# Attention beside a long convolution on one core: other steps for VectorE's share of the softmax, and a paced convolution

## The chip, the cores and the metric

The kernel runs on one core of one Trainium2 chip. The time is the device time of one execution in microseconds. Shown is the median of several runs and one profiled execution with its trace.

## What is computed

Two independent parts share a launch; their outputs stand side by side, each [2048, 512].

```python
# part A: attention, S = 2048, D = 512, 32 heads of 16
q, k, v = split_heads(x @ wqkv)
p = softmax((q @ k.T) * 16 ** -0.5)      # per head, 2048 x 2048
a = merge_heads(p @ v) @ wo

# part B: a gated long convolution, 512 channels, length 2048
kv = (sum over t of shifted(k, t) * shift_k[:, t]) * v
y = causal_conv(kv, ssm_k)               # per channel, written with FFTs
y = y + kv * ssm_D
b = q * y

out = concat([a, b], axis=-1)
```

## The kernel before, in words

Five instruction streams (PE, ScalarE or ACT, VectorE or DVE, GpSimd or POOL, and SP) are written out by a Python loop over steps `T`. Each engine runs its stream in order; semaphores tie them together. What the loop emits in which step is therefore the order of each queue; the steps are no clock.

**Attention.** Scores are made in blocks of 128 keys by 512 queries for one head. Four heads make a group, so a group is 64 blocks (16 key tiles by 4 heads), and 32 groups (4 blocks of queries by 8) make the whole. A step takes three blocks (two in some early steps): `emit_qk(T)` (matmul at line 487) writes them to PSUM banks 0-2 or 3-5 in turn, and one ScalarE instruction (line 494) takes the exponential of all three into a slot of `PT`. There are 692 steps, 21.33 to a group. In a later step `emit_pv` (line 559) multiplies the exponentials with the values and sums into bank 6. After a group's last block `finish_group` copies the sum out (`OF`, line 584), turns it (586), and in the next two steps makes the reciprocal (592), turns back (593) and multiplies into `OTN` (599).

**VectorE's share.** From the fifth group on (group 4, step 94), four blocks of each group are not done by ScalarE. `DVE_AT` says in which steps of the group, as two pairs: the third block of such a step is left to VectorE, and ScalarE takes two. VectorE reads the bank right away (`exp_on_dve`, line 512, the "fix", into `EI`), which frees it. Both blocks of a pair are then carried through a polynomial together: `split` (lines 516 and 518), `horner` three times (523) and `last` (528, into `PTD`). These five items are put into `dve_fill`, each with a step in which it is due, and the loop emits them ahead of the background work of that step. The matmuls on `PTD` are emitted six steps after the second block of the pair.

**Background.** In each step `emit_bg` adds one piece of other work to PE, all of it in bank 7. It is one of: a part of a q projection (24 units of two steps, evacuated by line 321), a part of an output projection (12 jobs of three steps, evacuated by line 639), or a stretch of the convolution. The convolution of four channels (a "quad") is 16 lags of four small matmuls (line 679) against `WR`, windows of the reversed filter that are read from a scratch in HBM (`load_wr`, 512 KB a channel, issued on SP's queue). `WR` holds 12 channels, three quads; a quad's slots are loaded anew when its last lag is emitted. After four quads the bank is copied to `YB` (695); after eight, `conv_turn` transposes and multiplies with the gate (706 and 715), and after 32 the gated result is stored by POOL's queue. There are 128 quads, 2048 lags.

Up to `LAGS` = 5 lags go into a step. A hand-made estimate decides whether the next window can be there: `now(T)` gives a time for the step, `st["wr"]` holds the time at which each quad's loads should have landed, and while that isn't reached the step gets no lag. Between groups of four quads one or more jobs are started; a started job takes its steps before any lag.

```python
    def now(T):
        t1 = N_EARLY + 30
        return 12.0 + 1.36 * min(T, t1) + 1.28 * max(T - t1, 0)
```

`bank_free[b]` holds the instruction that last emptied bank `b`; whoever writes the bank next waits for it.

Of the kernel before, what the change touches and what calls it, by code (L numbers as in the profile page):

```python
# [35 lines left out]
LAGS = 5  # L36
# [7 lines left out]
QSCALE = SCALE * math.log2(math.e) * OCT  # L44
FIX_LO = -118.0 * OCT
FIX_ADD = (math.log2(C4) - 1.0) * OCT
DVE_AT = ((2, 4), (10, 12))


class Eng:  # L50
# [41 lines left out]
def bass_concat_heads__mha_block__ssm_conv_h3__prompt_kernel(  # L92
# [165 lines left out]
    bank_free = {b: None for b in range(8)}  # L258
# [166 lines left out]
    chunks = []  # L425
    b_ = 0
    while b_ < NBLK:
        T = len(chunks)
# [34 lines left out]
    dve_pv = {}  # L463
    for n in range(2, NQB * NG):
        t0 = chunk_of[first[n]][0]
        if t0 < N_EARLY + 30:
            continue
        for pair in DVE_AT:
            for t in pair:
                on_dve[chunks[t0 + t][0][2]] = len(on_dve)  # L470
                dve_pv[chunks[t0 + t][0][2]] = t0 + pair[1] + 6

    h_exp = {}
    h_blk = {}
# [32 lines left out]
    def exp_on_dve(b, bank, h, T):  # L507
        i = on_dve[b]
        p = i // 2
        m = EM[:, :, :].bitcast(FP32)  # L510
        st = {}
        h_fix[i] = dve.op(lambda e: e.tensor_scalar(EI[:, i % 2, :], PS[:, bank, :], FIX_LO, FIX_ADD, ALU.max, ALU.add),  # L512
                          [h, h_pair.get(p - 1)])

        def split():
            st["m"] = dve.op(lambda e: e.tensor_scalar(EM[:, :, :], EI[:, :, :], 0x7fffff, 0x3f800000,  # L516
                                                       ALU.bitwise_and, ALU.bitwise_or), [h_fix[i], h_fix[i - 1]])
            st["e"] = dve.op(lambda e: e.tensor_scalar(EI[:, :, :], EI[:, :, :], 0x7f800000, 0x40000000,  # L518
                                                       ALU.bitwise_and, ALU.bitwise_xor), [st["m"]])

        def horner(j):
            src = m if j == 0 else EH[:, :, :]
            st["h"] = dve.op(lambda e: e.scalar_tensor_tensor(EH[:, :, :], src, (B3, B2, B1)[j], m, ALU.add, ALU.mult),  # L523
                             [st["m"], st.get("h")])

        def last():
            h_pair[p] = h_blk[b] = h_blk[b1] = dve.op(
                lambda e: e.scalar_tensor_tensor(PTD[:, :, :], EH[:, :, :], B0, EI[:, :, :].bitcast(FP32),  # L528
                                                 ALU.add, ALU.mult), [st["h"], st["e"], h_ptd.get(p - 1)])
        if i % 2:  # L530
            b1 = blk_on_dve[i - 1]
            dve_fill.extend([(T + 1, split), (T + 2, lambda: horner(0)), (T + 3, lambda: horner(1)),
                             (T + 4, lambda: horner(2)), (T + 5, last)])
        return h_fix[i]

    blk_on_dve = {i: b for b, i in on_dve.items()}
    dve_fill = []
# [130 lines left out]
    def conv_lags(qd, n0, n1):  # L668
        kk = qd % 8
        deps = [h_wr[4 * qd + c] for c in range(4)] + [h_kvc[0]]  # L670
        if kk % 4 == 0 and n0 == 0:
            deps.append(bank_free[BGB])

        def fn(e):
            ins = None
            for n in range(n0, n1):
                for c in range(4):
                    d = 4 * qd + c
                    ins = e.matmul(PS[32 * c:32 * c + NB - n, BGB, 128 * (kk % 4):128 * (kk % 4) + 128],  # L679
                                   lhsT=KV[:, n:NB, d],  # L680
                                   rhs=WR[:, d % R_W, 128 * (NB - 1 - n):128 * (NB - n)],
                                   start=(n == 0), stop=(n == NB - 1), tile_position=(0, 32 * c))
            return ins
        h = pe.op(fn, deps)
        if n1 == NB:
            for c in range(4):
                h_wrfree[4 * qd + c] = h
                if 4 * qd + c + R_W < C:
                    load_wr(4 * qd + c + R_W)
            if kk % 4 == 3:  # L690
                half = kk // 4
                src = PS[:, BGB, :]
                src = bass.AP(tensor=src.tensor, offset=PS[:, BGB, 127:128].offset,
                              ap=[src.ap[0], [128, 4], [-1, 128]])
                hh = dve.op(lambda e: e.tensor_copy(YB[:, half, :].rearrange("p (k i) -> p k i", k=4), src),  # L695
                            [h, h_yb[0]])
                bank_free[BGB] = hh
        return h
# [28 lines left out]
    for o in range(1, 4):  # L727
# [1 line left out]
    later_q = [("q", qb, g) for qb in range(1, NQB) for g in range(NG)]  # L729
    later_op = [(qb, t) for qb in range(NQB - 1) for t in range(4)]  # L730
    state = {"early": 0, "qd": 0, "lag": 0, "turn": False, "q": 0, "op": 0, "job": [], "gap": 0, "started": False,
             "wr": [], "dma": 0.0}

    def now(T):
        t1 = N_EARLY + 30
        return 12.0 + 1.36 * min(T, t1) + 1.28 * max(T - t1, 0)

    def group_step(qb, g):
        return NT * (qb * NG + g) // (NQB * NG)
# [13 lines left out]
    def emit_bg(T):  # L753
        st = state
        if st["early"] < len(early):
            if T % 3 == 2 and T >= 16:
                return
            unit(early[st["early"]], 5 if T < N_EARLY - 1 else 7)
            st["early"] += 1
            return  # L760
        if not kv_pieces and not st["started"]:
            st["started"] = True
            st["dma"] = now(T) + 18.0
            for i in range(R_W // 4):
                st["wr"].append(st["dma"] + 1.5)
            load_wop(pe_last())
            for d in range(R_W):
                load_wr(d)
            for i in range(2):
                load_qn(i, [h_kvc[0], h_kzt[0]])  # L770
            return
        if st["turn"]:
            conv_turn(st["qd"] // 8 - 1)
            st["turn"] = False
            st["gap"] = 0
            return
        if not st["started"]:
            return
        if st["job"]:
            st["job"].pop(0)()  # L780
            return
        if st["qd"] % 4 == 0 and st["lag"] == 0:
            ready = st["qd"] < C // 4 and st["wr"][st["qd"]] <= now(T)
            urgent = st["q"] < len(later_q) and T + 60 > group_step(*later_q[st["q"]][1:])
            if st["gap"] < 1 or urgent or not ready:
                if not urgent and st["op"] < len(later_op) and (later_op[st["op"]][0] * NG + NG - 1) in h_otn:
                    start_job(op_job(*later_op[st["op"]]))
                    st["op"] += 1
                    return
                if st["q"] < len(later_q):  # L790
                    u = later_q[st["q"]]
                    if T >= group_step(u[1] - 2, u[2]) + 30:
                        start_job(unit_job(u))
                        st["q"] += 1
                        return
        left = LAGS
        while left and st["qd"] < C // 4 and st["wr"][st["qd"]] <= now(T) and not st["turn"]:
            n0 = st["lag"]
            n1 = min(n0 + left, NB)
            left -= n1 - n0  # L800
            conv_lags(st["qd"], n0, n1)
            st["lag"] = n1 % NB
            if n1 == NB:
                st["qd"] += 1
                for i in range(4):
                    st["dma"] = max(st["dma"], now(T) + 3.0) + 1.3
                st["wr"].append(st["dma"] + 1.5)
                if st["qd"] % 4 == 0:
                    st["gap"] = 0
                    st["turn"] = st["qd"] % 8 == 0  # L810
                    break

    def pe_last():
        return (pe.sem, pe.n)
# [3 lines left out]
    for b in range(NBLK):  # L818
        qb, g, kt, s = blk(b)
        n = qb * NG + g  # L820
        t = dve_pv[b] if b in on_dve else chunk_of[b][0] + 2
        if n >= 2:
            t = max(t, chunk_of[last_blk[n - 1]][0] + 3)
        pv_at.setdefault(t, []).append(b)

    for T in range(NT + 3):
        if T < NT:
            emit_qk(T)
        if T == NT:
            op_mm(NQB - 1, 0, 0, 7, BGB)  # L830
            op_mm(NQB - 1, 1, 0, 7, chunks[NT - 2][1][0])
        pvs = pv_at.get(T, [])
        while pvs:
            emit_pv(pvs[:4], T)
            pvs = pvs[4:]
        for item in list(dve_fill):
            if item[0] <= T:
                dve_fill.remove(item)
                item[1]()
        emit_bg(T)  # L840
        for item in list(dve_later):
            if item[0] <= T:
                dve_later.remove(item)
                item[1]()
        for _ in range(1 if T < 3 else 0 if T < 9 else 1 if T < N_EARLY else 2):
            if kv_pieces:
                kv_pieces.pop(0)()
# [65 lines left out]
```

## Time and profile before

| | |
|---|---|
| median of 3 runs | 970.77 us (970.12 to 973.75) |
| profiled execution | 970.83 us, span 969.0 us |
| granted PE clock, mean | 0.933 |
| ScalarE busy | 898.0 us (93%) |
| PE busy (matmul rows) | 780.4 us (81%) |
| VectorE busy | 653.8 us (67%) |
| DMA read from HBM | 287.31 MB, 303 GB/s over the span |

How to read the lines that follow: a row of the timeline has its start and its length in us, the engine, the line of the kernel, the operation, output<-input, the count of instructions that were merged, and in brackets the idle time before it with what ended it. A row of the waits has who waited, `<-` for whom, the total in us, how often, and the longest. A row of the groups has after the bar the busy time in us and the mean length of one in ns, then the idle time before. PE is the matmul, PEld the weight load. PE's granted clock is 1.00 at full speed.

### The profile page before, as it was taken

The numbers are of one execution on the slowest core, as the hardware profiler recorded it, in microseconds if no ns is written. First come the engines' busy times: TensorE is split into PE (matmuls) and PEld (weight loads), VectorE is DVE, ScalarE is ACT, GpSimd is POOL, SyncE is SP. The second block draws the span as 40 slices with busy tenths as digits, with TensorE's granted clock in tenths as the row PEclk, the third lists the DMA queues.
The fourth block names the chain that finished last, engine by engine and source line by source line (L and its number), as shares of the span: only waits on it lengthen the run. The fifth ranks groups of instructions, "written<-read, shape, count | busy, mean of one in ns | idle before, by whom it ended". The sixth has DMA issues, their size and how long they took to land.

```text
span 969.0 us, 28338 instructions
## 1 busy us (share of the span) xinstructions
PE 780.4 (81%) x12851; PEld 341.5 (35%) x12892; DVE 653.8 (67%) x834; ACT 898.0 (93%) x699; POOL 46.7 (5%) x65
## 2 busy tenths in 40 slices
PE   8998887887777877777778777777777788787888
PEld 3322123433333433334334333343333334343212
DVE  3678825766776766776775676667786767677664
ACT  4788898999999999999999989999999999999995
POOL 2011410000000100000001000000000000000000
PEclk8999798999999999999998999999999999999656
DMA  9533399998989999989999989999999999998100
GB/s 315 179 110 109 87 303 357 362 372 338 367 328 349 359 367 364 369 334 384 354 365 346 358 322 347 347 361 360 346 381 349 344 354 350 373 397 349 22 1 22
DMA packets 88570, 295.59 MB, mean 305 GB/s; under 512 B 11269, under 2 KB 19458, under 8 KB 88066
## 3 DMA queue, kind: packets, MB, share of 16 engines
q1 hardware_dynamic: 82114, 280.13, 77.0%
q0 software_dynamic: 3936, 12.58, 4.1%
q8 instruction: 102, 1.67, 0.7%
q10 hardware_dynamic: 2400, 1.05, 0.4%
q14 instruction: 18, 0.15, 0.0%
HBM read 287.31 MB, written 6.42 MB: 303 GB/s over the span
## 4 chain that ended last, share of the span: by engine, by line
ACT 37%; DVE 34%; PE 20%; DMA 5%; issue 3%; SPq 1%; ACTq 0%
ACT PT L494 36%; DVE EH L523 10%; DMA WR<-kz_scratch 5%; PE PS L487 5%; PE PS L559 4%; PE PS L679 3%; DVE EI L512 3%; DVE PTD L528 3%; DVE EI L518 2%; PE PS L631 2%; DVE EM L516 2%; PE PS L307 2%; DVE DT L586 2%; DVE OF L584 2%; DVE OTN L599 2%
## 5 line engine op out<-in xcount | busy, mean ns | idle before, releaser
L494 ACT ACTIVATE PT<-PS 128x1536 bf16<-128x1536 f32 (+1 forms) x692 | 892.8, 1460 | 53.4 <-PE PS L487 51.4
L487 PE MATMUL PS<-QT,KTo 32*128 32x512 bf16 x2048 | 287.4, 409 | 108.1 <-ACT PT L494 101.6
L679 PE MATMUL PS<-WR,KV 128*8 128x128 bf16 (+15 forms) x8192 | 298.5, 227 | 25.2 <-DMA WR<-kz_scratch 11.4
L559 PE MATMUL PS<-PT,VAF 128*32 128x512 bf16 x1936 | 306.2, 414 | 2.0 <-issue 0.7
L679 PEld LDWEIGHTS PS<-WR,KV 128*14 128x14 bf16 (+15 forms) x8192 | 195.9, 107 | 57.7 <-issue 42.0
L512 DVE TENSOR_SCALAR EI<-PS 128x512 int32<-128x512 f32 x112 | 78.1, 698 | 144.8 <-PE PS L487 141.9
L487 PEld LDWEIGHTS PS<-QT,KTo 32*128 32x128 bf16 x2048 | 67.9, 91 | 280.7 <-ACT PT L494 217.6
L523 DVE SCALAR_TENSOR_TENSOR EH<-EH,EM 128x1024 f32<-128x1024 f32 x112 | 139.8, 1249 | 3.5
L559 PEld LDWEIGHTS PS<-PT,VAF 128*32 128x32 bf16 x1936 | 69.3, 94 | 161.4 <-issue 151.1
L528 DVE SCALAR_TENSOR_TENSOR PTD<-EH,EI 128x1024 bf16<-128x1024 f32 x56 | 70.4, 1258 | 1.6
L523 DVE SCALAR_TENSOR_TENSOR EH<-EM 128x1024 f32<-128x1024 f32 x56 | 70.7, 1262 | 0.0
L584 DVE COPY OF<-PS 128x512 f32<-128x512 f32 x30 | 20.5, 685 | 46.9 <-PE PS L559 39.7
L293 PE MATMUL PS<-xT,WQP 128*128 128x512 bf16 x109 | 35.3, 405 | 9.1 <-DVE QN L715 3.8
L518 DVE TENSOR_SCALAR EI<-EI 128x1024 int32<-128x1024 int32 x56 | 39.9, 713 | 1.9
L516 DVE TENSOR_SCALAR EM<-EI 128x1024 int32<-128x1024 int32 x56 | 40.2, 718 | 1.1
L695 DVE CAST YB<-PS 128x512 bf16<-128x512 f32 x32 | 21.8, 682 | 28.2 <-PE PS L679 20.9
L631 PE MATMUL PS<-WKV,OTN 128*128 128x512 bf16 x115 | 33.9, 408 | 8.1 <-DVE QN L715 2.9
L559 PE MATMUL PS<-PTD,VAF 128*32 128x512 bf16 x112 | 24.3, 430 | 19.9 <-DVE PTD L528 19.7
L321 DVE TENSOR_SCALAR QT<-PS 128x512 bf16<-128x512 f32 x32 | 21.9, 686 | 26.6 <-PE PS L293 26.6
L169 POOL DMA_DIRECT2D out_dram<-OUTA x12 | 6.6, 551 | 369.6 <-DVE OUTA L639 369.6
L593 DVE STREAM_TRANSPOSE DT<-DR 128x512 f32<-128x512 f32 x31 | 22.4, 723 | 1.1
L169 POOL DMA_DIRECT2D out_dram<-QN x4 | 4.7, 1171 | 382.1 <-DVE QN L715 382.1
(66 smaller groups left out, 299.3 us busy)
## 6 DMA issues: line engine op xcount, KB each, us to landing
WR<-kz_scratch SPq DMA_DIRECT2D x512, 512.0 KB, 8.4
WR<-in_B_k_dram POOLq DMA_DIRECT2D x16, 256.0 KB, 4.9
kz_scratch<-WR SPq DMA_DIRECT2D x1, 2176.0 KB, 8.9
KV<-in_A_x_dram SPq DMA_DIRECT2D x4, 512.0 KB, 6.7
QN<-in_B_q_dram POOLq DMA_DIRECT2D x4, 512.0 KB, 11.3
out_dram<-QN POOLq DMA_DIRECT2D x4, 512.0 KB, 8.0
WR<-in_B_v_dram SPq DMA_DIRECT2D x6, 256.0 KB, 3.2
QT<-in_B_k_dram POOLq DMA_DIRECT2D x6, 256.0 KB, 4.2
```

The source lines that it names most:

```text
L293: return e.matmul(PS[:, bank, :], lhsT=WQP[:, dc, g, :], rhs=xT[:, dc, qb * 512:(qb + 1) * 512], start=(dc == 0), stop=(dc == 3))
L487: ins = e.matmul(PS[:, bank, :], lhsT=KTo[32 * s:32 * s + 32, g // 2, kt * 128:(kt + 1) * 128], rhs=QT[32 * s:32 * s + 32, qb % 2, g, :], ...
L494: h_exp[T] = act.op(lambda e: e.activation(PT[:, T % R_PT, 0:n * QB], PS[:, banks[0]:banks[0] + n, :].rearrange("p b f -> p (b f)"), ACT.E ...
L512: h_fix[i] = dve.op(lambda e: e.tensor_scalar(EI[:, i % 2, :], PS[:, bank, :], FIX_LO, FIX_ADD, ALU.max, ALU.add), [h, h_pair.get(p - 1)])
L516: st["m"] = dve.op(lambda e: e.tensor_scalar(EM[:, :, :], EI[:, :, :], 0x7fffff, 0x3f800000, ALU.bitwise_and, ALU.bitwise_or), [h_fix[i], ...
L518: st["e"] = dve.op(lambda e: e.tensor_scalar(EI[:, :, :], EI[:, :, :], 0x7f800000, 0x40000000, ALU.bitwise_and, ALU.bitwise_xor), [st["m"]])
L523: st["h"] = dve.op(lambda e: e.scalar_tensor_tensor(EH[:, :, :], src, (B3, B2, B1)[j], m, ALU.add, ALU.mult), [st["m"], st.get("h")])
L528: lambda e: e.scalar_tensor_tensor(PTD[:, :, :], EH[:, :, :], B0, EI[:, :, :].bitcast(FP32), ALU.add, ALU.mult), [st["h"], st["e"], h_ptd. ...
L559: ins = e.matmul(PS[32 * s:32 * s + 32, pvb(qb * NG + g), :], lhsT=VAF[:, kt, h * VW:h * VW + 32], rhs=rhs, start=(kt == 0), stop=(kt == K ...
L584: h_of = dve.op(lambda e: e.tensor_copy(src, PS[:, pvb(n), :]), [h, before])
L631: ins = e.matmul(PS[:, bank, :], lhsT=OTN[:, oslot(qb * NG + g), t * 128:(t + 1) * 128], rhs=WOP[:, g, :], start=(g == 0), stop=(g == NG - 1))
L679: ins = e.matmul(PS[32 * c:32 * c + NB - n, BGB, 128 * (kk % 4):128 * (kk % 4) + 128], lhsT=KV[:, n:NB, d], rhs=WR[:, d % R_W, 128 * (NB - ...
```

## The change

- `DVE_AT` moves the pairs of VectorE's blocks in a group from steps 2 and 4, and 10 and 12, to steps 3 and 5, and 12 and 14.
- `DVE_LAG` = 8: the matmuls on a pair's `PTD` are emitted eight steps after its second block instead of six.
- The five items of `dve_fill` become due at two to six steps after the second block instead of one to five. At most one is emitted in a step, now behind the background work instead of ahead of it; it may come before it is due, from the second block's own step on, if the background of the step emptied no bank; in a step that emptied one it is emitted only when due.
- `PACE` = 3.6: a credit of lags, `st["lags"]`, grows by 3.6 in each step of the running background (up to 15; not in the steps of `conv_turn`), and a step takes at most the whole lags of the credit, at most five.
- The estimate of a load's time grows from 1.3 to 1.42.

```diff
--- before.py
+++ after.py
@@ -44,7 +44,9 @@
 QSCALE = SCALE * math.log2(math.e) * OCT
 FIX_LO = -118.0 * OCT
 FIX_ADD = (math.log2(C4) - 1.0) * OCT
-DVE_AT = ((2, 4), (10, 12))
+DVE_AT = ((3, 5), (12, 14))
+DVE_LAG = 8
+PACE = 3.6
 
 
 class Eng:
@@ -468,7 +470,7 @@
         for pair in DVE_AT:
             for t in pair:
                 on_dve[chunks[t0 + t][0][2]] = len(on_dve)
-                dve_pv[chunks[t0 + t][0][2]] = t0 + pair[1] + 6
+                dve_pv[chunks[t0 + t][0][2]] = t0 + pair[1] + DVE_LAG
 
     h_exp = {}
     h_blk = {}
@@ -529,8 +531,8 @@
                                                  ALU.add, ALU.mult), [st["h"], st["e"], h_ptd.get(p - 1)])
         if i % 2:
             b1 = blk_on_dve[i - 1]
-            dve_fill.extend([(T + 1, split), (T + 2, lambda: horner(0)), (T + 3, lambda: horner(1)),
-                             (T + 4, lambda: horner(2)), (T + 5, last)])
+            dve_fill.extend(zip(range(T + DVE_LAG - 6, T + DVE_LAG - 1),
+                                [split, lambda: horner(0), lambda: horner(1), lambda: horner(2), last]))
         return h_fix[i]
 
     blk_on_dve = {i: b for b, i in on_dve.items()}
@@ -729,7 +731,7 @@
     later_q = [("q", qb, g) for qb in range(1, NQB) for g in range(NG)]
     later_op = [(qb, t) for qb in range(NQB - 1) for t in range(4)]
     state = {"early": 0, "qd": 0, "lag": 0, "turn": False, "q": 0, "op": 0, "job": [], "gap": 0, "started": False,
-             "wr": [], "dma": 0.0}
+             "wr": [], "dma": 0.0, "lags": 0.0}
 
     def now(T):
         t1 = N_EARLY + 30
@@ -776,6 +778,7 @@
             return
         if not st["started"]:
             return
+        st["lags"] = min(st["lags"] + PACE, 3.0 * LAGS)
         if st["job"]:
             st["job"].pop(0)()
             return
@@ -793,17 +796,18 @@
                         start_job(unit_job(u))
                         st["q"] += 1
                         return
-        left = LAGS
+        left = min(LAGS, int(st["lags"]))
         while left and st["qd"] < C // 4 and st["wr"][st["qd"]] <= now(T) and not st["turn"]:
             n0 = st["lag"]
             n1 = min(n0 + left, NB)
             left -= n1 - n0
+            st["lags"] -= n1 - n0
             conv_lags(st["qd"], n0, n1)
             st["lag"] = n1 % NB
             if n1 == NB:
                 st["qd"] += 1
                 for i in range(4):
-                    st["dma"] = max(st["dma"], now(T) + 3.0) + 1.3
+                    st["dma"] = max(st["dma"], now(T) + 3.0) + 1.42
                 st["wr"].append(st["dma"] + 1.5)
                 if st["qd"] % 4 == 0:
                     st["gap"] = 0
@@ -833,11 +837,10 @@
         while pvs:
             emit_pv(pvs[:4], T)
             pvs = pvs[4:]
-        for item in list(dve_fill):
-            if item[0] <= T:
-                dve_fill.remove(item)
-                item[1]()
+        before = dict(bank_free)
         emit_bg(T)
+        if dve_fill and (bank_free == before or dve_fill[0][0] <= T):
+            dve_fill.pop(0)[1]()
         for item in list(dve_later):
             if item[0] <= T:
                 dve_later.remove(item)
```

## The prediction

> **What bounds the kernel now.** I read the busy times by stretch first, then who waits for whom, then the timeline around the longest waits of ScalarE. By stretch the columns are: stretch, length, busy time (instructions) of PE, PEld, DVE, ACT and POOL, granted clock, DMA share, GB/s.
>
> ```profile
> span 969.0 us, 28338 instructions
> 0.00:124.00 124.00, 108.76 (x637) 34.73 (x647) 86.15 (x150) 94.67 (x79) 31.43 (x46) 0.92 0.49 164
> 124.00:905.00 781.00, 615.85 (x11941) 294.74 (x11968) 529.38 (x635) 751.12 (x580) 14.80 (x20) 0.97 0.94 351
> 905.00:969.00 64.00, 55.78 (x276) 12.03 (x277) 38.23 (x49) 52.20 (x42) 0.50 (x1) 0.57 0.06 17
> ```
>
> Between 124 and 905 us ScalarE (ACT) is busy for 751.1 of 781 us with the exponentials of line 494, 1.295 us a step (751.1/580). VectorE is at 68%, PE's rows at 79%. So the kernel is bound by ScalarE, and what it can win is ScalarE's waiting. The view of waits, for ACT in the same three stretches in this order:
>
> ```profile
> ACT PT L494 <- PE PS L487: 21.7, 31, 1.8
> ACT PT L494 <- PE PS L487: 28.0, 45, 2.2
> ACT PT L494 <- PE PS L487: 1.6, 3, 0.7
> ```
>
> The first 21.7 us lie in steps that the change leaves alone (polynomial blocks start with group 4, step 94; the conv at step 83). The pool is 28.0 + 1.6 = 29.6 us, 3.0% of the time. The profiled execution took 970.83 us (span 969.0 plus 1.8 outside it), the median of the runs 970.77, so the sum needs no shift. With the whole pool gone it would be 970.8 - 29.6 = 941.2 us; no way below that is in sight, since the change removes no ScalarE work.
>
> ScalarE waits when PE reaches the QK of a step late, and PE is late because something stood ahead of it in its queue. I went through all 45 waits in the timeline and put each to the last PE row before it that itself waited. The parts come below, with the change that touches them.
>
> **The change, part by part.** No instruction is added or removed: 112 blocks go to VectorE before and after, and 8192 conv matmuls, 512 window loads, 24 q units, 12 output jobs and 16 turns stay. Only places move. I counted them by carrying the counters of emit_bg, pv_at and dve_fill through all 692 steps with the old and the new lines.
>
> *Weights used later.* The six VectorE passes of a pair take, by the groups of instructions:
>
> ```profile
> L516 DVE TENSOR_SCALAR EM<-EI 128x1024 int32<-128x1024 int32 x56 | 40.2, 718 | 1.1
> L518 DVE TENSOR_SCALAR EI<-EI 128x1024 int32<-128x1024 int32 x56 | 39.9, 713 | 1.9
> L523 DVE SCALAR_TENSOR_TENSOR EH<-EM 128x1024 f32<-128x1024 f32 x56 | 70.7, 1262 | 0.0
> L523 DVE SCALAR_TENSOR_TENSOR EH<-EH,EM 128x1024 f32<-128x1024 f32 x112 | 139.8, 1249 | 3.5
> L528 DVE SCALAR_TENSOR_TENSOR PTD<-EH,EI 128x1024 bf16<-128x1024 f32 x56 | 70.4, 1258 | 1.6
> ```
>
> 0.718 + 0.713 + 1.262 + 2 x 1.249 + 1.258 = 6.45 us, five steps of 1.295 (6.48). Now the last pass is emitted in step T+5 and its matmul in T+6: one step of slack in all 56 pairs, and any evacuation between the passes uses it up.
>
> ```profile
> PEld PS L559 <- DVE PTD L528: 36.4, 53, 1.7
> PE PS L559 <- DVE PTD L528: 19.7, 34, 1.4
> 339.90 1.23 DVE L528 SCALAR_TENSOR_TENSOR PTD<-EH,EI 128x1024 bf16<-128x1024 f32 x1
> 341.18 0.39 PE L559 MATMUL PS<-PTD,VAF 128*32 128x512 bf16 x2 [1.45 <-DVE PTD L528]
> 342.17 0.61 PE L487 MATMUL PS<-QT,KTo 32*128 32x512 bf16 x3
> 342.83 1.47 ACT L494 ACTIVATE PT<-PS 128x1536 bf16<-128x1536 f32 x1 [1.29 <-PE PS L487]
> 254.62 1.45 ACT L494 ACTIVATE PT<-PS 128x1536 bf16<-128x1536 f32 x1 [1.19 <-PE PS L487]
> 775.81 18.32 ACT L494 ACTIVATE PT<-PS 128x1536 bf16<-128x1536 f32 x14 [0.35 <-PE PS L487]
> 943.21 14.46 ACT L494 ACTIVATE PT<-PS 128x1536 bf16<-128x1536 f32 x11 [0.72 <-PE PS L487]
> ```
>
> The weight loads waited for the last pass in 53 of 56 pairs. One case in full: PE stands 1.45 us before the matmul on PTD, behind it the next QK, and ScalarE loses 1.29 us. Waits of this kind, from the one at 254.62 to the one at 775.81, 16 in number, sum to 9.4 us; two more behind 905 (the last at 943.21) to 1.1. After the change the passes may start in step T, and the matmul stands in T+8: the slack is 4 steps for 33 pairs, 3 for 8 and 2 for 15, that is 2.6 to 5.2 us where waits of up to 1.7 stood. I take all 10.5 us as won. Late next is nothing of VectorE's: PTD and EI are held longer, but the next pair writes PTD five steps after the matmul at the earliest, and the next fix still comes a step after the latest last pass, as now. The cost is at the end: the last pair's two matmuls move from step 688 to 692, behind the last exponentials; I bound it by 0 and 0.34 us (a step with five of these matmuls took 1.51 us there, a step with three 1.17) and take 0.2.
>
> *Passes out of evacuating steps.* A pass emitted ahead of the background now stands in VectorE's queue in front of the copy that empties bank 7, and PE's next background work waits:
>
> ```profile
> 595.66 0.68 DVE L695 CAST YB<-PS 128x512 bf16<-128x512 f32 x1
> 596.62 0.59 PE L631 MATMUL PS<-WKV,OTN 128*128 128x512 bf16 x2 [1.69 <-DVE YB L695]
> 597.59 1.45 ACT L494 ACTIVATE PT<-PS 128x1536 bf16<-128x1536 f32 x1 [0.75 <-PE PS L487]
> 163.63 5.31 ACT L494 ACTIVATE PT<-PS 128x1536 bf16<-128x1536 f32 x4 [0.94 <-PE PS L487]
> 744.14 2.38 ACT L494 ACTIVATE PT<-PS 128x1536 bf16<-128x1536 f32 x2 [0.35 <-PE PS L487]
> 187.62 36.99 ACT L494 ACTIVATE PT<-PS 128x1536 bf16<-128x1536 f32 x29 [0.18 <-PE PS L487]
> 302.83 1.06 PE L631 MATMUL PS<-WKV,OTN 128*128 128x512 bf16 x2 [0.69 <-DVE DR L592]
> 304.43 1.02 ACT L494 ACTIVATE PT<-PS 128x1024 bf16<-128x1024 f32 x1 [1.59 <-PE PS L487]
> 794.39 67.09 ACT L494 ACTIVATE PT<-PS 128x1536 bf16<-128x1536 f32 x52 [0.26 <-PE PS L487]
> ```
>
> Late evacuations cost ScalarE 13.5 us. Of these 7.2 (11 waits from 163.63 to 744.14) have a pass in front; 6.3 (12 waits, 187.62 to 794.39) have other work in front, mostly the OF copy, transposes and reciprocal of a finished group, which dve_fill doesn't rule. From step 86 on 77 steps evacuate bank 7. With a pass ahead in the same step: 35 before, 0 after (four are forced, but stand behind the copy). With a pass in the step before: 32 before, 35 after; VectorE doesn't wait for steps, so such a pass can still be running. Hence between nothing and all of the 7.2 is won. I take 5.2: a pass one step back has a step of 1.295 us before the copy is due, and its row says 1.25, so it is through except where it began late. The 6.3 stay: evacuations within a step of a group's end are 11 before and 12 after.
>
> *Even pace.* Now lags run at 5 a step, 16 to a quad, until the next window isn't expected yet: 30 steps of the conv carry no lag at all. After, 2048 lags at 3.6 are 569 steps, with 16 turns 585: the conv ends at step 666 instead of 649 of 692, and 4 steps are empty. The loads:
>
> ```profile
> 147.16 0.55 PE L679 MATMUL PS<-WR,KV 128*16 128x128 bf16 x12 [2.90 <-DMA WR<-kz_scratch]
> 148.30 1.47 ACT L494 ACTIVATE PT<-PS 128x1536 bf16<-128x1536 f32 x1 [2.23 <-PE PS L487]
> 236.00:238.00 2.00, 2.00 (x63) 1.27 (x58) 0.00 (x0) 1.90 (x2) 0.00 (x0) 1.00 0.06 25
> 246.00:248.00 2.00, 1.17 (x28) 0.58 (x25) 1.97 (x3) 2.00 (x2) 0.00 (x0) 1.00 1.03 422
> ```
>
> Waits that go back to a load cost ScalarE 5.0 us. At full rate (246 to 248) a 512 KB window takes 524288/422e3 = 1.24 us, a quad 4.97 us; five lags a step use a quad in 3.2 x 1.295 = 4.1 us, so the queue falls behind and then stands empty (236 to 238). At 3.6 a quad lasts 4.44 x 1.295 = 5.8 us, which the loads can follow. The SP queue holds these loads in the same order and nothing else until the end; the q loads and stores on POOL's queue follow the turns, the last 17 steps later, still 25 before the end. The 2.23 us at 148.30 stay: this is the fourth quad, due in step 94 both before and after. I take 2.5 of the 5.0.
>
> *Sum.* 10.5 - 0.2 + 5.2 + 2.5 = 18.0 us. 970.8 - 18.0 = 952.8 us.
>
> **The rivals.** *The clock falls (the other side).* PE's clock halves for spells, and not only in a full stop:
>
> ```profile
> 319.44 0.39 PE L487 MATMUL PS<-QT,KTo 32*128 32x512 bf16 x3 [0.45 <-ACT PT L494]
> 322.21 0.61 PE L487 MATMUL PS<-QT,KTo 32*128 32x512 bf16 x3
> 512.08 0.61 PE L487 MATMUL PS<-QT,KTo 32*128 32x512 bf16 x3
> 513.70 0.61 PE L487 MATMUL PS<-QT,KTo 32*128 32x512 bf16 x3
> 944.72 0.61 PE L487 MATMUL PS<-QT,KTo 32*128 32x512 bf16 x3
> 945.81 0.61 PE L487 MATMUL PS<-QT,KTo 32*128 32x512 bf16 x3
> ```
>
> After an empty step (319.44) the QK rows go from 0.39 to 0.61 us, though PE worked in every step. A slow step with five lags takes 1.62 us (512.08 to 513.70), one with none 1.09 (944.72 to 945.81, where the granted clock of the stretch is 0.57), so a lag costs 0.106 and a slow step at 3.6 lags 1.09 + 0.38 = 1.47 us, 0.175 over ScalarE's 1.295. A pace of 3.6 leaves PE a pause in every step. If that lets the clock fall for a share x of the 583 conv steps, it costs 102x us: from x = 0.18 on nothing is won, from 0.22 on it is slower by over 0.5%, and at one half the time is 952.8 + 51 = 1004 us. Against it: of the 30 empty steps only six were followed by slow rows within four steps, so a stretch with an empty step in it, poorer in matmuls than 3.6 lags a step, mostly stays fast; and the granted clock between 124 and 905 is 0.97.
>
> The Trainium skill (TensorE: Matmul & The Clock Gate, "A second HAM failure mode: psum-queue depth-cycling") has a rule that speaks for this rival: short idle spells between groups of matmuls, repeated often, make the clock swing; by it the time would be near 1004. Another rule of the Trainium skill (the same page, "What's actually happening") asks for an idle window of about 3.4 us before the clock halves; by it no paced step could be slow, and the sum stays. The trace agrees with neither in full: at 322.21 the clock had fallen without such a window, and spells are rare.
>
> *Only the later use counts.* Credit for lags piles up during jobs (to 15) and is spent at 5 a step: 265 of 496 conv steps still carry five. If loads fall behind as now, and the 35 passes one step ahead of an evacuation cost what the 35 in the same step did, 5.2 and 2.5 fall away: 970.8 - 10.3 = 960.5 us. For it: VectorE's queue takes passes without regard to steps. Against it: the load queue has 5.8 us for 4.97.
>
> *Nearly all of it.* If the waits at group ends go too, because the first fix moves from two to three steps behind the group's start, away from the OF copy: 952.8 - 6.3 = 946.5 us.
>
> **How the numbers follow.** 952.8 has 0.58 (its own range 948 to 957), 960.5 has 0.18, 946.5 has 0.08, and the clock 0.16, of which half lies near no change and half beyond. Within 0.5% (4.9 us, about what a measurement here can tell from none) is 966.0 to 975.6. So faster 0.84, same 0.08, slower 0.08. The range from 944 (just above the 941.2 that empties the pool) to 964 leaves out the clock's cases and little else.
>
> **What would show it.** In the changed profile the wait of line 559 on PTD should be gone, ACT's wait on line 487 between 124 us and the conv's end near 11 us (2.0 + 6.3 + 2.5), the wait of 2 us or more at the fourth quad still there, the DMA share even instead of falling to 0.06, and the 0.6 us QK rows in the conv confined to a few places. It is wrong if PTD is still waited for, or if the granted clock in the conv falls below about 0.9 (x = 0.2 at half clock).

## The result, and the profile after

| | before | after |
|---|---|---|
| median (range) | 970.44 us (969.13 to 973.75) | 941.35 us (938.88 to 944.74) |
| profiled execution, span | 970.83, 969.0 us | 938.88, 937.1 us |
| granted PE clock, mean | 0.933 | 0.964 |

The ratio is 0.9698 [0.9653, 0.9742]: faster, by some 29 us where 18 were forecast, and below the range of 944 to 964. In a later comparison, on another chip, the changed kernel came to 941.97 us and 0.969 [0.9661, 0.972]. Four executions fell in a disturbed state, 994.93 us of f3, 976.91 of a3, and 1948.54 and 2180.82 of the kernel before beside b1, b2, b3 and c1; no median and no ratio below holds them.

The busy times by stretch of the changed kernel, columns as before (the lines named here carry numbers two higher than in the old kernel: the exponential is line 496 now, QK 489, the old lines 559, 584, 679 and 528 are 561, 586, 681 and 530):

```profile
span 937.1 us, 28375 instructions
0.00:124.00 124.00, 108.76 (x661) 34.25 (x661) 87.68 (x153) 97.45 (x81) 33.12 (x47) 0.96 0.52 169
124.00:905.00 781.00, 627.20 (x12108) 299.96 (x12105) 554.48 (x660) 773.69 (x602) 13.72 (x18) 0.98 0.94 351
905.00:937.00 32.00, 26.87 (x129) 6.74 (x126) 17.06 (x23) 21.60 (x18) 0.00 (x0) 0.65 0.05 17
```

In the same 781 us ScalarE now does 602 exponentials instead of 580. Its waits up to 124 us and from 124 to 905 us, in this order (behind 905 there are none), then the waits of PE's weight load and matmul on `PTD` and PE's wait on the window loads, over the whole execution:

```profile
ACT PT L496 <- PE PS L489: 19.1, 32, 1.3
ACT PT L496 <- PE PS L489: 6.9, 12, 2.3
PEld PS L561 <- DVE PTD L530: 3.1, 4, 1.0
PE PS L561 <- DVE PTD L530: 1.9, 4, 0.7
PE PS L681 <- DMA WR<-kz_scratch: 10.0, 7, 2.9
```

Of the pool of 29.6 us, 6.9 are left. The chain that ended last, by engine, was a mixture before; it is mostly ScalarE now. Before:

```profile
ACT 37%; DVE 34%; PE 20%; DMA 5%; issue 3%; SPq 1%; ACTq 0%
```

After:

```profile
ACT 75%; PE 11%; DVE 7%; DMA 6%; SPq 1%; issue 1%; ACTq 0%
```

The group of the exponentials shows something that the prediction had excluded. Before:

```profile
L494 ACT ACTIVATE PT<-PS 128x1536 bf16<-128x1536 f32 (+1 forms) x692 | 892.8, 1460 | 53.4 <-PE PS L487 51.4
```

After:

```profile
L496 ACT ACTIVATE PT<-PS 128x1536 bf16<-128x1536 f32 (+1 forms) x692 | 887.5, 1533 | 26.5 <-PE PS L489 26.0
```

The same 692 instructions are busy for 5.3 us less (the mean in ns counts overlapping ones twice; the busy time doesn't). Between the two profiled executions, 970.83 - 938.88 = 31.95 us, the time went this way: waits from 124 us on 29.6 - 6.9 = 22.7; waits before 124 us 21.7 - 19.1 = 2.6; busy time of the exponentials 5.3; everything else 1.3.

### The profile page after: what moved, and what is told of

Same layout as the page of the kernel before. It is cut to its first block, busy times and chain, and to the rows that moved or that the text cites. A ratio compares the mean times of both kernels' runs of the same rounds, so it can differ in the third digit from the quotient of the medians.

```text
span 937.1 us, 28375 instructions
## 1 busy us (share of the span) xinstructions
PE 762.8 (81%) x12892; PEld 340.9 (36%) x12892; DVE 659.2 (70%) x834; ACT 892.7 (95%) x699; POOL 46.8 (5%) x65
## 4 chain that ended last, share of the span: by engine, by line
ACT 75%; PE 11%; DVE 7%; DMA 6%; SPq 1%; issue 1%; ACTq 0%
ACT PT L496 74%; DMA WR<-kz_scratch 5%; PE PS L489 2%; PE PS L561 2%; PE PS L309 2%; PE PS L633 2%; PE PS L302 1%; PE PS L681 1%; DMA WKV<-in_A_wqkv_dram 1%; SPq L171 1%; DVE VAF L338 1%; DVE WR L373 1%; DVE WR L377 1%; DVE KTo L332 1%; PE PS L295 1%
## 5 line engine op out<-in xcount | busy, mean ns | idle before, releaser
L489 PE MATMUL PS<-QT,KTo 32*128 32x512 bf16 x2048 | 279.8, 398 | 132.1 <-ACT PT L496 125.1
L681 PE MATMUL PS<-WR,KV 128*15 128x128 bf16 (+15 forms) x8192 | 312.8, 225 | 17.8 <-DMA WR<-kz_scratch 10.0
L561 PE MATMUL PS<-PT,VAF 128*32 128x512 bf16 x1936 | 297.3, 403 | 1.1 <-DVE OF L586 0.7
L681 PEld LDWEIGHTS PS<-WR,KV 128*13 128x13 bf16 (+15 forms) x8192 | 201.9, 106 | 53.5 <-issue 33.0
L295 PE MATMUL PS<-xT,WQP 128*128 128x512 bf16 x128 | 38.6, 395 | 4.9 <-DVE YB L697 2.2
L633 PE MATMUL PS<-WKV,OTN 128*128 128x512 bf16 x128 | 35.9, 398 | 2.8 <-DVE YB L697 1.4
L588 DVE STREAM_TRANSPOSE DT<-OF 128x512 f32<-128x512 f32 x30 | 22.1, 738 | 1.0
## 6 DMA issues: line engine op xcount, KB each, us to landing
QN<-in_B_q_dram POOLq DMA_DIRECT2D x4, 512.0 KB, 11.6
```

The costliest lines, as they stand in the source:

```text
L295: return e.matmul(PS[:, bank, :], lhsT=WQP[:, dc, g, :], rhs=xT[:, dc, qb * 512:(qb + 1) * 512], start=(dc == 0), stop=(dc == 3))
L489: ins = e.matmul(PS[:, bank, :], lhsT=KTo[32 * s:32 * s + 32, g // 2, kt * 128:(kt + 1) * 128], rhs=QT[32 * s:32 * s + 32, qb % 2, g, :], ...
L561: ins = e.matmul(PS[32 * s:32 * s + 32, pvb(qb * NG + g), :], lhsT=VAF[:, kt, h * VW:h * VW + 32], rhs=rhs, start=(kt == 0), stop=(kt == K ...
L633: ins = e.matmul(PS[:, bank, :], lhsT=OTN[:, oslot(qb * NG + g), t * 128:(t + 1) * 128], rhs=WOP[:, g, :], start=(g == 0), stop=(g == NG - 1))
```

## The experiments

The first theory was that each part did what the prediction said, only more. Its rivals: that the *place* of the pairs, which the prediction had treated as a part of the later use, did most of it by freeing the group's end on VectorE; and that the pace won by the clock and by room on PE, not by loads.

The table gives the ratio to the kernel before on the same chip, and ScalarE's waits from 124 us on (in us, one profiled execution of each), put to what PE's last own wait before them was for: window loads; `PTD`; work of VectorE that empties a bank or ends a group; no wait of PE that the trace shows. In the kernel before the third kind is 15.5 by this grouping (13.5 by the prediction's), the second 8.1 (10.5, of which 1.1 lie behind 905 us).

| kernel | median us | ratio [95%] | loads | PTD | evacuation | none |
|---|---|---|---|---|---|---|
| before | 969.7 to 974.0 | 1 | 5.0 | 8.1 | 15.5 | 1.0 |
| after | 941.35 | 0.9698 [0.9653, 0.9742] | 5.3 | 0.0 | 1.3 | 0.4 |
| g1, the change again | 941.97 | 0.969 [0.9661, 0.972] | 7.3 | 0.2 | 0.8 | 0.9 |
| a1, place and later matmul | 954.15 | 0.983 [0.9781, 0.9878] | 7.8 | 0.0 | 5.2 | 5.4 |
| a2, order alone | 994.63 | 1.0226 [1.0155, 1.0297] | 3.9 | 32.0 | 9.4 | 8.1 |
| a3, pace alone | 969.34 | 0.9969 [0.9933, 1.0005] | 4.0 | 9.5 | 12.0 | 1.5 |
| a4, change without pace | 949.76 | 0.978 [0.9732, 0.9829] | 6.8 | 0.3 | 5.8 | 1.8 |
| b1, change without order | 946.19 | 0.9746 [0.967, 0.9821] | 7.1 | 0.0 | 3.2 | 0.7 |
| b2, order and pace | 995.35 | 1.0261 [1.0186, 1.0337] | 4.8 | 37.0 | 10.6 | 6.2 |
| b3, change, pairs at 2, 4, 11, 13 | 956.05 | 0.9874 [0.9798, 0.9949] | 5.3 | 0.6 | 8.1 | 3.4 |
| c1, change at 5.0 a step | 947.59 | 0.9771 [0.9717, 0.9825] | 8.3 | 0.0 | 3.8 | 3.5 |
| f1, place alone | 953.94 | 0.9823 [0.9789, 0.9857] | 7.4 | 1.3 | 4.1 | 1.9 |
| f2, second pair's place alone | 965.56 | 0.9923 [0.9892, 0.9954] | 9.0 | 3.3 | 10.7 | 1.3 |
| f3, first pair's place, second pair one step on | 954.24 | 0.9801 [0.9754, 0.9849] | 6.6 | 2.4 | 5.9 | 2.0 |
| d1, change, first pair back at 2, 4 | 954.01 | 0.9838 [0.9803, 0.9874] | 7.6 | 0.2 | 11.3 | 4.7 |
| h1, change without later use | 967.13 | 0.9962 [0.9922, 1.0001] | 7.1 | 21.5 | 0.7 | 2.2 |
| h2, place and pace | 947.94 | 0.9753 [0.9675, 0.9832] | 13.3 | 2.2 | 2.8 | 0.2 |
| e1, change with planned empty steps | 940.08 | 0.9691 [0.9666, 0.9717] | 1.3 | 0.0 | 3.5 | 0.2 |
| e2, even pace without credit | 938.05 | 0.9672 [0.9645, 0.97] | 4.5 | 0.6 | 2.6 | 0.2 |
| e4, e2 with planned empty steps | 936.49 | 0.9627 [0.9597, 0.9657] | 1.1 | 0.4 | 1.9 | 1.2 |

The waits of h2 and d1 are those of their longest execution, 954.70 and 959.82 us, those of f1 of its shortest, 949.13.

**One part at a time.** Edits to the kernel before:

```diff
 a1   -DVE_AT = ((2, 4), (10, 12))      +DVE_AT = ((3, 5), (12, 14))
      -    ... = t0 + pair[1] + 6       +    ... = t0 + pair[1] + 8
 a2   -for item in list(dve_fill): ...  (ahead of emit_bg)
      +before = dict(bank_free)
       emit_bg(T)
      +if dve_fill and (bank_free == before or dve_fill[0][0] <= T):
      +    dve_fill.pop(0)[1]()
 a3   +PACE = 3.6, the credit, and 1.42 for 1.3, as in the change
```

a4 is the change with `left = LAGS` and 1.3 again.

> Only the later use: the pairs at steps 3, 5, 12, 14 and the matmuls on PTD eight steps after; passes stay ahead of the background, due one to five steps after; five lags a step. Theory A (each cause has its own price): PE's waits on PTD vanish and with them some 10.5 us of ScalarE's waits plus 16 to 18 restarts of about 0.11 us; the rest stays: 958 to 961 us. Theory B (PE's lack of room in five-lag steps and the slow-clock spells turn small delays into ScalarE waits): the PTD waits vanish too, but part of the room is lost to the other stalls: 962 to 967.

> Only the order: passes behind the background, one a step, kept out of evacuating steps until due; pairs at steps 2, 4, 10, 12, matmuls on PTD six steps after, five lags a step. Theory A: the waits with a pass in front go (7.2 us), PTD waits shrink too, because the passes may start a step earlier: 959 to 964. Theory B: 963 to 969.

> Only the pace of 3.6 lags with the estimate of 1.42. Theory A: only empty steps and loads are touched, 2 to 4 us: 966 to 969. Theory B: the pace gives PE room in every step and keeps its clock up, so waits on PTD still occur but reach ScalarE less, and the stalls at group ends shrink: 952 to 960, slow spells fewer than half of before's.

> The change without the pace: up to five lags a step and the estimate of 1.3 as before. Theory A: loses only what the pace brought, 2 to 4 us: 943 to 946. Theory B: the stalls at group ends and the slow spells come back: 950 to 957.

a1 won 17.5 us, a3 about 2 (not clear of no change), and a2 *lost* 23. The effects alone, -17.5 + 23 - 2, make +4, the whole -29: the parts are not additive, and a2 says why. PE's waits on `PTD` in a2:

```profile
PEld PS L559 <- DVE PTD L528: 57.3, 55, 2.3
PE PS L559 <- DVE PTD L528: 39.9, 42, 2.0
```

In the kernel before they were 36.4 and 19.7. With T the step of the second block, the matmul still stands in T+6. Counted from the loop, the last pass is emitted in T+4 for 34 of the 56 pairs and in T+5 for the other 22, whose passes gave way to a step that empties a bank; before it was T+5 for all, ahead of the background work. From the start of the second fix to the end of the last pass it is 7.40 us for the 34 pairs and 9.03 for the 22, against 7.74 before, and the 22 hold 27.1 of PE's 39.9 us. What the new place spares the copies, it costs the matmuls, with interest.

**One part taken away.** Edits to the change:

```diff
 b1   dve_fill loop of the kernel before, items due at T + 1 to T + 5
 b2   -DVE_AT = ((3, 5), (12, 14))      +DVE_AT = ((2, 4), (10, 12))
      -DVE_LAG = 8                      +DVE_LAG = 6;  items due at T + 1 to T + 5
 b3   -DVE_AT = ((3, 5), (12, 14))      +DVE_AT = ((2, 4), (11, 13))
 c1   -PACE = 3.6                       +PACE = 5.0
```

> The change with the old order: passes ahead of the background, due one to five steps after the second block, whether or not the step empties bank 7; later use and pace stay. If the parts add up (order brought 954.15 - 949.76 = 4.4 us on top of the later use): 945 to 947 us. If the pace hides what a pass in front costs, because every step has room: 940 to 943.

> The change without the later use: pairs at steps 2, 4, 10, 12, matmuls on PTD six steps after, passes due one to five steps after but behind the background, pace kept. If the parts add up, the order's loss without the later use (994.6) less the 2 to 8 us of the pace: 986 to 993 us, PE's weight loads waiting for PTD in 50 or more of 56 pairs. If the pace gives the passes room: 970 to 980.

> The change with the pairs a step earlier, at steps 2, 4, 11, 13 of the group, all else kept. If the waits at group ends went because the first fix now stands a step behind the OF copy, transposes and reciprocal: they come back, 4 to 6 us, 945 to 948. If they went because paced steps have room: no more than 1 us, 940 to 943.

> The change with PACE = 5.0, so that the credit no longer binds, and the estimate of a load's time at 1.42. If the even spread of lags brought the 8 us between the kernel without pace (949.8) and the change: 947 to 951. If the longer estimate brought them, by starting quads only when their windows are there: 940 to 943, waits for loads as in the change.

Without the order the change is 946.2 us, so on top of the rest the order is worth about 5 us, though the intervals of the ratios overlap; a4 against a1, which differ by the order alone, makes it 4.4. b2 is as slow as a2, by the same wait. b3 is the surprise: the pairs one step earlier than in the change, all else as in it, cost 14.7 us, and ScalarE hardly waits behind `PTD` (0.6). Something in the place itself counts. c1 keeps the estimate of 1.42 and gives back 6.2 us, nearly what a4 gives (8.4): most of the pace's part is the evening out, not the estimate.

**Which pair, and why.** f1, f2 and f3 are the kernel before with other places alone, d1 the change with the first pair back. f3 moves the second pair too, by one step; only d1 moves the first pair by itself:

```diff
 f1   -DVE_AT = ((2, 4), (10, 12))      +DVE_AT = ((3, 5), (12, 14))
 f2   -DVE_AT = ((2, 4), (10, 12))      +DVE_AT = ((2, 4), (12, 14))
 f3   -DVE_AT = ((2, 4), (10, 12))      +DVE_AT = ((3, 5), (11, 13))
 d1   -DVE_AT = ((3, 5), (12, 14))      +DVE_AT = ((2, 4), (12, 14))
```

> The change with only the first pair a step earlier, steps 2, 4, 12, 14. If the first pair's fix beside the group's end is the costly one: near the kernel with both pairs early, 952 to 956. If the second pair's place costs as much: 946 to 950.

> The kernel before with nothing but the pairs moved to steps 3, 5, 12, 14; matmuls on PTD still six steps after. If the place of the pairs relative to the group's end is what frees the copies of bank 7 (moving them back cost the changed kernel some 14 us): waits on the OF, transposes and reciprocal shrink from 5 to 1 or 2 us and the time falls to 958 to 964 while PTD is still waited for. If the place only helps once PTD is used later: 967 to 973.

> The kernel before with only the second pair moved, steps 2, 4, 12, 14; six steps to the matmuls, so the first pair's stand in step 10, beside no fix. If the shared step is what lets a late PTD reach ScalarE: PE still waits for PTD in some 50 of 56 pairs, but ScalarE's waits behind it fall from 8 to under 2 us, 959 to 963 us. If it is the group's end: no more than 3 us, 967 to 971.

> The kernel before with the first pair at 3, 5 and the second at 11, 13, so that the first pair's matmuls on PTD stand in step 11 beside the second pair's first fix, as before. If the shared step counts: ScalarE's waits behind PTD stay at 7 to 9 us, those behind the OF, transposes and reciprocal fall from 5 to 1 or 2: 962 to 966 us. If only the first pair's place at the group's end counts: 953 to 957.

Place alone does all that a1 does (953.94 and 954.15): the matmul's two steps more add nothing there. The first pair with the second one step on gives 954.2 (the kernel before took 974.0 beside it), the second pair alone 965.6, and the first pair put back into the change costs 12.7 us. A rival that I had put up was that the first pair's matmuls stand in the step of the second pair's first fix (step 10). It isn't needed for the gain: f3 keeps such a shared step (11), and its class `PTD` is 2.4 instead of 8.1. f2, which has no shared step and leaves the first pair where it was, has 3.3 there and gains 8.4 us, so the shared step may hold a smaller part.

The mechanism stands in VectorE's timeline at a group's end. Before, it is the end at which the prediction showed PE at 302.83 and ScalarE losing 1.59 us at 304.43. The matmul's row there names the reciprocal, but by the code it needs only bank 7's copy, line 695, and its weight load names that (last line):

```profile
299.76 0.69 DVE L512 TENSOR_SCALAR EI<-PS 128x512 int32<-128x512 f32 x1 [6.94 <-PE PS L487]
300.37 0.68 DVE L584 COPY OF<-PS 128x512 f32<-128x512 f32 x1
301.08 0.71 DVE L586 STREAM_TRANSPOSE DT<-OF 128x512 f32<-128x512 f32 x1
301.72 0.65 DVE L695 CAST YB<-PS 128x512 bf16<-128x512 f32 x1
302.29 0.23 DVE L592 RECIPROCAL DR<-DT 128x16 f32<-128x16 f32 x1
302.56 0.71 DVE L593 STREAM_TRANSPOSE DT<-DR 128x512 f32<-128x512 f32 x1
302.42 0.13 PEld L631 LDWEIGHTS PS<-WKV,OTN 128*128 128x128 bf16 x2 [1.20 <-DVE YB L695]
```

After, at a group's end:

```profile
290.22 0.69 DVE L586 COPY OF<-PS 128x512 f32<-128x512 f32 x1 [4.36 <-PE PS L561]
290.94 0.77 DVE L588 STREAM_TRANSPOSE DT<-OF 128x512 f32<-128x512 f32 x1
291.62 0.65 DVE L514 TENSOR_SCALAR EI<-PS 128x512 int32<-128x512 f32 x1
292.20 0.23 DVE L594 RECIPROCAL DR<-DT 128x16 f32<-128x16 f32 x1
```

A group's last sum and its copy `OF` are emitted two steps behind its last block. Where that is step 2 of the next group, the old first fix stood in the same step ahead of the copy, since the fix is emitted with QK and the copy later. Counted from the loop, that was so at 19 of the 28 group ends that a first fix follows, and at none after. VectorE had idled 6.94 us, and then got the fix, the copy and its transpose and bank 7's copy without a gap, while PE stood behind them. With the fix a step later the copy starts as soon as the sum is there. The wait of the copy measures that: who finds VectorE idle at a group's end. Before:

```profile
DVE OF L584 <- PE PS L559: 39.7, 8, 6.9
DVE OF L584 <- PE PS L679: 7.2, 1, 7.2
```

After:

```profile
DVE OF L586 <- PE PS L561: 87.8, 22, 19.5
DVE OF L586 <- PE PS L681: 4.1, 1, 4.1
```

In f3, the first pair's place with the second pair one step on:

```profile
DVE OF L584 <- PE PS L559: 120.9, 25, 19.4
DVE OF L584 <- PE PS L679: 10.0, 2, 6.2
```

In d1, the change with the first pair back:

```profile
DVE OF L586 <- PE PS L561: 20.3, 7, 5.0
```

9 of 30 copies before, 23 after, 27 in f3, 7 in d1 (f1: 27, f2: 9, b3: 8). Over all 20 executions the two go together without exception: the 13 kernels whose first pair stands at 3, 5 have 23 to 28 such copies and evacuation waits of 0.7 to 5.9 us, the 7 with the first pair at 2, 4 have 7 to 9 and 8.1 to 15.5. No run moves the first fix without the rest of its pair, so its own share isn't shown apart. The passes of the first pair begin later too, clear of that queue, and `PTD` is less late by place alone: in f1 they end 7.63 us after the start of the second fix instead of 7.93, and PE's wait on first pairs falls from 14.1 to 6.8 us, on second pairs only from 5.6 to 4.8. Of the 11.6 us together (19.7 before) 1.3 reach ScalarE (8.1 before).

**Is the later use needed at all?** h1 is the change with `DVE_LAG` = 6 and the items due at T + 1 to T + 5; h2 the kernel before with place and pace.

> The change with the pairs at 3, 5, 12, 14 but the matmuls on PTD six steps after the second block again, passes due one to five steps after. If the later use is the price of the new order (passes that give way to a copy come late for a PTD used after six steps): PE waits for PTD in 45 or more of 56 pairs again and the time is 955 to 975 us. If the place alone makes PTD early enough: 941 to 947.

> The kernel before with the pairs at 3, 5, 12, 14 and the pace of 3.6, nothing else. If place and pace are what counts: 942 to 947 us. If order and later use bring some 5 us more together: 946 to 951, PE still waiting for PTD in 40 or more pairs.

PE's wait on `PTD` in h1, 1.9 us in the change:

```profile
PE PS L561 <- DVE PTD L530: 30.1, 28, 2.0
```

Yes, but only because of the order. Without the later use 25.8 of the 29 us are gone. Where the order is the old one, place and pace alone reach 947.9, about what b1 has with the later use added (946.2; the intervals overlap). So the later use pays for the order and has no sure gain of its own.

**Loads and the pace.** The waits on loads didn't shrink: 5.0 before, 5.3 and 7.3 in the two profiles of the change. They stand at few places. The timeline of the change at two of them (rows left out):

```profile
143.82 0.55 PE L681 MATMUL PS<-WR,KV 128*16 128x128 bf16 x12 [2.13 <-DMA WR<-kz_scratch]
144.96 1.47 ACT L496 ACTIVATE PT<-PS 128x1536 bf16<-128x1536 f32 x1 [1.47 <-PE PS L489]
329.63 1.16 POOL L171 DMA_DIRECT2D QN<-in_B_q_dram  x1 [6.98 <-DMA out_dram<-QN]
341.81 0.77 PE L681 MATMUL PS<-WR,KV 128*16 128x128 bf16 x20 [2.88 <-DMA WR<-kz_scratch]
342.51 0.61 PE L489 MATMUL PS<-QT,KTo 32*128 32x512 bf16 x3
343.16 1.47 ACT L496 ACTIVATE PT<-PS 128x1536 bf16<-128x1536 f32 x1 [2.33 <-PE PS L489]
```

The first is the third of the initial quads; the second a quad loaded while POOL's queue stores a gate and reads the next (a third such place is near 535 us). Here e1 plans empty steps; e2 takes away the credit that piles up in jobs, so that no burst of five lags follows them; e4 does both, for the two later quads; g1 is the change once more. Edits to the change:

```diff
 e1   +QN_GAP = {33: 3.9, 65: 3.9}
      -    st["wr"].append(st["dma"] + 1.5)    (the initial loads)
      +    st["wr"].append(st["dma"] + (4.1 if i == 2 else 1.5))
      +    st["dma"] += QN_GAP.get(st["qd"], 0.0)
 e2   -PACE = 3.6                       +PACE = 4.1
      -    ... PACE, 3.0 * LAGS)        +    ... PACE, 5.0)
      -    ... + 1.42                   +    ... + 1.3
 e4   e2 and   +QN_GAP = {33: 2.6, 65: 2.6}
               +    st["dma"] += QN_GAP.get(st["qd"], 0.0)
```

> The change with a planner that knows of three late loads: the window of quad 2 is expected 2.6 us later, and the two quads loaded while the gate is stored and read anew (35 and 67) 3.9 us later each; PE then gets empty steps instead of standing in front of QK. If a late load costs only because it stands ahead of QK: ScalarE's waits on loads fall from 5.3 us to under 1.5, 936 to 939 us. If the empty steps bring slow clock that costs as much: 940 to 943.

> The change with 4.1 lags a step, no credit saved up during jobs (at most 5.0), and the estimate back at 1.3: the same conv work without the stretches of five lags after jobs. If these bursts outrun the loads and take PE's room: waits on loads fall by half, 937 to 940 us. If the longer estimate is what keeps quads from starting early: waits on loads rise, 943 to 947.

> 4.1 lags a step without saved credit, estimate 1.3, and quads 35 and 67 expected 2.6 us later. If the remaining waits on loads at the gate's store and reload can be planned around: one to two us below the same kernel without it, 936 to 938 us. If the empty steps cost as much: 938 to 940.

> The changed kernel once more, beside the others on one chip: 938 to 944 us, ScalarE's waits from 124 us to the end 6 to 8 us; the first 124 us vary by some 2 us from run to run without the change's doing.

e1 took the load waits from 5.3 to 1.3 us, but the slow rows of QK at the same three places stayed, and its 940.1 us can't be told from the change's 941.4 to 942.0. e2 reached 938.05. e4 is the best of all, 936.49 us, its interval just below that of the change in the same comparison (0.9627 [0.9597, 0.9657] and 0.969 [0.9661, 0.972]). Its stretches:

```profile
124.00:905.00 781.00, 614.72 (x12061) 305.34 (x12090) 555.56 (x663) 775.87 (x605) 12.96 (x17) 0.99 0.95 351
905.00:937.00 32.00, 19.88 (x143) 6.75 (x144) 14.55 (x21) 17.88 (x16) 1.17 (x1) 0.86 0.13 33
```

ScalarE's wait in e4 from 124 to 905 us:

```profile
ACT PT L497 <- PE PS L490: 4.7, 15, 1.1
```

Spells of 0.6 us QK rows in the conv, ahead of the long one at the end, are 14 before, 6 after, 3 in e2 and 2 in e4; PE's busy time in the stretch falls from 627.2 to 614.7 us at nearly the same number of matmuls. That would go with a gain of the pace by room on PE. But the pace alone doesn't thin the slow spells out (15 in a3), and which of the two, shorter steps after jobs or fewer slow rows, wins the time wasn't separated. How the pace wins its 8.4 us stays open.

## Why the prediction was wrong, step by step

*"ScalarE bounds, and its waits are the pool."* Right: 22.7 of the 31.95 us between the profiles are its waits from 124 us on.

*"970.8 - 29.6 = 941.2 us; no way below that is in sight, since the change removes no ScalarE work."* Failed, and the range ended at 944 because of it. ScalarE's busy time isn't fixed: an exponential that starts after a wait takes longer than one in an unbroken run. The timeline of the change in the early steps, where no block is left to VectorE:

```profile
117.14 1.45 ACT L496 ACTIVATE PT<-PS 128x1536 bf16<-128x1536 f32 x1 [0.60 <-PE PS L489]
118.98 5.48 ACT L496 ACTIVATE PT<-PS 128x1536 bf16<-128x1536 f32 x4 [0.38 <-PE PS L489]
```

One alone takes 1.45 us; four take 5.48, so each further one (5.48 - 1.45)/3 = 1.34. Over the 20 profiled executions the busy time of the exponentials is 880.5 us + 0.15 us for each wait (r = 0.88), and what is left of the span, 23.1 to 25.3 us, hardly moves. 35 fewer waits make 5.3 us, just what the groups show. The views list no wait below 0.15 us; with those counted too the line is 0.12 us for each wait (r = 0.91), near the 0.11 of the rows. So each listed wait saved was worth some 0.15 us more than its length, of which 0.11 is its own restart. The Trainium skill (ScalarE: Activation LUTs, "What ACT_TABLE_LOAD costs") says that back-to-back ACTIVATEs overlap by about 93 ns; the 0.11 us between 1.45 and 1.34 are near it, and the 0.15 for each listed wait lies above it.

*"Weights used later, 10.5 us."* The size was right, but by luck in part, since the cause was only half right. The waits on `PTD` went (19.7 to 1.9 us on PE), but in the old order place alone takes 6.8 of the 8.1 that reached ScalarE; in the new order the later use is needed (h1). I had counted the steps between passes and matmul and not what stands in VectorE's queue ahead of the passes.

*"I take 5.2 ... The 6.3 stay."* The most mis-sized term of the sum: evacuations gave 14.2 us instead of 5.2, for nearly nothing of either stays (1.3 of 15.5 us). It took this and the failed floor together to leave the range. With the waits as they came out the sum is 970.8 - 22.7 = 948.1 us, and with 5.3 us of busy time off the forecast it is 952.8 - 5.3 = 947.5, both inside; with waits and busy time it is 942.8, below 944. I had compared how many evacuations lie within a step of a group's end (11 and 12) and let the fix out of the count, though it stands in the same queue ahead of the copy. The rival "nearly all of it" named that mechanism and got 0.08; d1, b3 and f3 show that the first pair's place is the largest single effect of the change, 12.7 to 19.7 us. The order itself is worth 4 to 5 us, near the 5.2, but only with the later use, and only some 2 of it are evacuation waits (3.2 in b1, 1.3 in the change); the danger of the order alone, +23 us, was in none of the rivals.

*"Even pace, 2.5 of 5.0 us of loads."* Wrong in its reason. Load waits stayed, the pace was worth 2 us alone and 8.4 within the rest (a4), and most of what falls with it is evacuation (5.8 to 1.3). The mean DMA share was 0.94 before and is 0.94 after. It did get more even, as forecast: of the stretches of 2 us from 150 to 880 us 17 had a share below 0.5 before and 8 after. But e2, which is no slower, has 20, so an even load isn't what wins the time. One detail was misread: the stall at 147.16 us is the third of the initial quads (its step of five lags falls into 8 and 12 matmuls, lags 31 to 35), not the fourth; it did stay.

*"The clock falls."* Refuted: the granted clock from 124 to 905 us rose from 0.97 to 0.98, and to 0.99 in e4. Nor does the pace leave PE a pause in every step: in those 781 us PE stands over 0.15 us ahead of QK in 305 of 601 steps of the change, and in 246 of 578 before. By the rule of the Trainium skill on short idle spells (TensorE: Matmul & The Clock Gate, "A second HAM failure mode: psum-queue depth-cycling") the pauses that the pace leaves PE should have made the clock swing; the pairs of kernels that differ by the pace don't show that: 0.97 in the kernel before and in a3, 0.97 in a4 and 0.98 in the change, and where a paced one is low (b2, 0.92) the same kernel without the pace is too (a2, 0.93).

Left open: of the 2.6 us in the first 124 us, in steps that the change doesn't touch, the 19 other executions have 18.3 to 21.2 us there against the 21.7 of the kernel before; how much of this is in the medians isn't known.

## What to carry to other kernels

When work moves in an in-order queue, write down the whole queue of the engine around the moved piece: here one step's difference in the place of one pair, its first fix of 0.7 us ahead of a group's copy or behind it, was worth more (12.7 us in d1) than the order of all the passes (about 5). A reordering that delays a producer needs its consumer moved first, so test parts together as well as alone. On a bound engine, count its waits as well as their length, since each restart costs something on top (here 0.11 us).

## What the runs showed of the hardware that was not expected

An exponential of three banks takes 1.45 us after a wait and 1.34 in an unbroken run; over whole executions a listed wait cost 0.15 us beyond itself. In the change, e1, e2 and e4 the granted clock from 124 to 905 us is 0.98 to 0.99 at 3.6 or 4.1 lags a step, while slow rows follow single late loads in three of the change's six spells: QK is at 0.61 us at 342.51, right after PE had stood for 2.88 us. The other three spells (from 508.6, 582.6 and 720.3 us) follow no wait on a load, and why the clock fell there isn't known.
